# Weight shapes priced in a planner, the first expert's list read before the last block's rows are stored

## The chip, the cores and the metric

The kernel runs on one core of a Trainium2 chip. The metric is the device time of one execution in microseconds; a kernel's time is the median of its runs. The core has five engines that run side by side and meet at semaphores: TensorE (PE; PEld is its weight load), VectorE (DVE), ScalarE (ACT), GpSimd (POOL) and SyncE (SP, which here only issues DMAs).

## What is computed

```python
# q, k, v, f_logit: (4, 8, 768, 48) float32
for t in range(S):                       # gated linear attention
    state = f[:, :, t, :, None] * state + einsum('bhd,bhe->bhde', k[:, :, t], v[:, :, t])
    y[:, :, t] = einsum('bhd,bhde->bhe', q[:, :, t], state)
x = y as 3072 rows of 384                # row = batch * 768 + t
h = x @ w_in                             # dense layer, 384 -> 2048 -> 384
x = (maximum(h, 0) + alpha * minimum(h, 0)) @ w_out
logits = x @ w_gate                      # 8 experts, 384 rows each
for idx in argsort(-logits.flatten()):   # greedy: best pair of row and expert first
    row, e = idx // 8, idx % 8
    if row is free and expert e has fewer than 384 rows: give row to e
out[rows of e] = maximum(x[rows of e] @ w1[e], 0) @ w2[e]   # 384 -> 1024 -> 384
```

## The kernel before

**A planner.** The Python code does not issue instructions directly. A recorder (its one line, L212 before and L215 after, is what the profile shows for nearly all instructions) collects each with what it reads and writes, a modelled cost, and a due time given by `with self.at(...)`. `schedule()` then writes them out engine by engine: at each step the instruction that can start first by the model, ties going to the earlier due time. Where the model sees PE idle, `fill()` puts in products with a matrix `ones` that nobody reads (L1670 before, L1723 after). The order on each engine is therefore fixed when the kernel is built, and a changed constant can move instructions anywhere. `AHEAD` (L47) says how many of the first expert's eight weight tiles are asked for ahead of its gather.

**Attention** runs in 24 chunks. A chunk's products on PE are of three shapes of weights: the k.q products (64 rows by 128 columns of weights, `bank<-early 64*128`), the y products and the state products (128 rows by 64 columns, `128*64`), and transposes by the matrix `ident` and the gate's products, which use the full 128 by 128.

**The dense layer** takes blocks of 384 rows as attention finishes them. Values are split in a high and a low part, so a full-precision product is three PE passes of 384 columns. Eight tiles hold the hidden weights, eight the project weights; each is built early on from the inputs by DVE, ACT and POOL (integer steps on `raw` and `early`, then `weights<-early`, one of whose steps, the split, may go to DVE or POOL as the planner finds). The hidden products are `bank<-rounded,weights`, the project products `bank<-weights,hidden` or, for rows still to be split, `bank<-weights,rounded`. The rows go to a DRAM tensor `x2d` (3072 by 384).

**The experts.** For each expert a chain on DVE and PE finds the threshold of its logits (`seek`, in steps of 12 small PE products `bank<-late 128x16`, one with `pairs`, one with `ok`), takes its rows, and makes a list of their numbers (`lists`: 24 small PE products in three groups of 8, then `idx`). POOL gathers the 384 listed rows from `x2d` with three indirect DMAs, `expert_x` transposes them (three groups of three PE transposes `bank<-ident,common`), and ACT and DVE split them; then come the hidden and the project products. The next expert's chain, list, gather and transposes stand among the products of the expert before it.

**The hand-over** from the dense layer to the first expert: the last block's logits are computed ahead of its rows, so the first expert's list is made while PE still does the last block's 144 project products (`ffn1_rows`). Those rows go to ACT, to `x2d`, and only then may the gather read `x2d`. SP issues, in this order: three weight tiles, the last two stores of rows to `x2d`, a tiny DMA `mark` that waits for the gathered rows, and the other weight tiles.

Of the kernel before, what the change touches and what calls it, by code (L numbers as in the profile page):

```python
# [32 lines left out]
BT = 3  # L33
BK = BT * C
NB = NT // BT
SEG = C + 1
# [13 lines left out]
AHEAD = 3  # L50
# [29 lines left out]
URGENT = 80.0  # L80
WINDOW, BUSY = 10240 / 3, 3060.0
# [53 lines left out]
class Op:  # L135
    def __init__(self, idx, engines, calls, prio):
# [3 lines left out]
        self.extra = 0.0  # L140
# [5 lines left out]
class Plan:  # L146
# [59 lines left out]
    def record(self, engines, method, a, k, slack=0.0):  # L206
# [121 lines left out]
    def schedule(self):  # L328
# [12 lines left out]
        mm, hw, dma = [0.0, 0.0], 600.0, [0.0, 0.0]  # L341

# [23 lines left out]
        for _ in ops:  # L366
# [267 lines left out]
class Kernel:  # L634
# [28 lines left out]
    def constants(self, cp):  # L663
# [19 lines left out]
        with self.at(PAIRS):  # L683
# [31 lines left out]
        nc.gpsimd.iota(self.jpv[:, :, 1], pattern=[[0, NT]], base=0, channel_multiplier=1,  # L715
                       allow_small_or_imprecise_dtypes=True)
# [183 lines left out]
    def s2(self, i):  # L900
        nc, a = self.nc, self.A[i]
        n = HP * SEG
        for name, dec in (("k", a["qr"][:, 1:n + 1].rearrange("p (g t) -> p g t", g=HP)[:, :, 1:]),
# [3 lines left out]
            nc.vector.tensor_tensor(t, a[name], dec, OP.mult)  # L907

# [15 lines left out]
    def s3k(self, i):  # L924
# [6 lines left out]
        for g in range(HP):  # L931
            nc.tensor.transpose(p[:, g * 128:(g + 1) * 128], a["kT"][:, g, :], self.ident)
# [33 lines left out]
    def s4s(self, i):  # L966
# [5 lines left out]
        for g in range(HP):  # L972
            for s in range(2):
                r = slice(s * 64, s * 64 + 64)
# [123 lines left out]
    def ffn1_rows(self, G, store):  # L1098

        for t in range(BT):  # L1100
# [5 lines left out]
            store(t, r, None)  # L1106

# [261 lines left out]
    def lists(self, idx, pos, acc):  # L1369

        nc, wp = self.nc, self.rp
        g = wp.tile([128, NT, 3], F32, name="pg", bufs=1)
# [24 lines left out]
        nc.vector.tensor_scalar(idx, pp, float(N - 1), None, op0=OP.min)  # L1397
# [46 lines left out]
    def gather(self, idx):  # L1444
        xg = [self.gw.tile([128, DM], F32, name="g", bufs=3) for a in range(3)]
        for a in range(3):
            self.nc.gpsimd.indirect_dma_start(out=xg[a], out_offset=None, in_=self.x2d,
# [62 lines left out]
    def flag(self):  # L1510
# [3 lines left out]
        ok = self.rp.tile([128, HP + E], BF, name="okp", bufs=1)  # L1514
        nc.vector.tensor_scalar(ok[:, :HP], self.pmin, PMIN, None, op0=OP.is_ge)
        nc.vector.tensor_scalar(ok[:, HP:], self.inc[:, :, NT - 1], float(CAP), None, op0=OP.is_equal)
        p = self.bank()
        nc.tensor.matmul(p[:, :HP + E], self.ones, ok, start=True, stop=True)
        s = self.rp.tile([128, 1], F32, name="oks", bufs=1)
        nc.vector.tensor_reduce(s, p[:, :HP + E], axis=AX.X, op=OP.add)  # L1520
        self.bad = self.cp.tile([128, 1], I32, name="bad")
        nc.vector.tensor_scalar(self.bad, s, 128.0 * (HP + E) - 0.5, None, op0=OP.is_lt)
# [329 lines left out]
```

## Time and profile before

| | |
|---|---|
| median of 3 runs | 847.98 us (847.36 to 849.97) |
| profiled execution, its own time | 851.19 us |
| its span in the trace | 849.30 us |
| granted PE clock, mean | 0.989 of full speed |
| PE busy | 820.0 us, 97% |
| DVE busy | 564.8 us, 66% |
| ACT, POOL busy | 349.6, 113.9 us |

The profiled execution is 3.21 us above the median, and its time holds 1.89 us outside the span. [...]

### The profile page before, as it was taken

Reading aid. Unit: us, or ns where it says so; the run is one execution under the profiler, and the core shown is the slowest. Engines: PE = TensorE matmul, PEld = TensorE weight load, DVE = VectorE, ACT = ScalarE, POOL = GpSimd, SP = SyncE. Lnnn points to the kernel's source line nnn. Section 1 sums busy time; section 2 is a strip of 40 time slices with the busy share of each in tenths; the row PEclk is TensorE's granted clock in tenths of the full one; section 3 lists DMA queues with packets and bytes.
Section 4 is the critical chain, followed back from the end, with each engine's and each line's share of the span. In section 5 each row is a group of like instructions: output and inputs, shape, how many; then the busy total and the mean of one; then the engine's idle time right before and its main releaser. Section 6 shows DMA issues by size and latency. Waiting matters only on the chain. (4 is left out here: it accounts for less than half of the span.)

```text
span 849.3 us, 16038 instructions
## 1 busy us (share of the span) xinstructions
PE 820.0 (97%) x6122; PEld 756.5 (89%) x6122; DVE 564.8 (66%) x1308; ACT 349.6 (41%) x742; POOL 113.9 (13%) x105
## 2 busy tenths in 40 slices
PE   6999989999999999999999999999999999999995
PEld 3687889999999999999999999888788999899995
DVE  6899976977866966966975754655767658452220
ACT  3577665355555355555455443420122212222220
POOL 3111011210200200300300000000202302311211
PEclk7999999999999999999999999999999999999998
DMA  8895202599889688988878770003878775687400
GB/s 177 221 315 135 48 20 75 136 289 281 231 274 292 136 291 256 236 278 279 248 237 290 251 240 29 1 10 134 312 277 329 316 288 183 246 314 230 164 28 33
DMA packets 92792, 172.60 MB, mean 203 GB/s; under 512 B 31674, under 2 KB 61378, under 8 KB 92706
## 3 DMA queue, kind: packets, MB, share of 16 engines
q1 hardware_dynamic: 89490, 162.04, 60.0%
q0 software_dynamic: 3072, 9.44, 3.2%
q8 instruction: 50, 0.82, 0.4%
q14 instruction: 36, 0.29, 0.1%
q10 hardware_dynamic: 144, 0.01, 0.0%
HBM read 111.69 MB, written 59.77 MB: 202 GB/s over the span
## 5 line engine op out<-in xcount | busy, mean ns | idle before, releaser
L212 PE MATMUL bank<-rounded,weights 128*128 128x384 f32 (+1 forms) x1740 | 354.4, 344 | 1.2 <-POOL weights L212 0.5
L212 PE MATMUL bank<-weights,rounded 128*128 128x392 f32 (+1 forms) x1620 | 325.1, 344 | 3.0 <-ACT weights L212 2.3
L212 PEld LDWEIGHTS bank<-rounded,weights 128*128 128x128 f32 (+1 forms) x1740 | 302.4, 187 | 7.7 <-issue 2.3
L212 PEld LDWEIGHTS bank<-weights,rounded 128*128 128x128 f32 x1620 | 287.5, 189 | 5.6 <-issue 3.2
L212 ACT ACTIVATE rounded<-bank 128x384 fp32r<-128x384 f32 x110 | 54.1, 492 | 201.1 <-PE bank L212 188.4
L212 DVE TENSOR_TENSOR early<-early 128x384 fp32r<-128x384 f32 (+2 forms) x196 | 120.0, 629 | 16.1 <-ACT early L212 15.1
L212 PEld LDWEIGHTS bank<-early 128*64 128x64 f32 (+2 forms) x1696 | 98.3, 153 | 20.9 <-issue 10.4
L212 PE MATMUL bank<-early 128*64 128x128 f32 (+3 forms) x1696 | 110.2, 269 | 2.7 <-DVE early L212 1.5
L212 DVE SCALAR_TENSOR_TENSOR common<-common,rest,bank 128x384 f32<-128x384 f32 x128 | 77.9, 608 | 47.1 <-ACT common L232 46.1
L212 ACT ACTIVATE early<-early 128x384 fp32r<-128x384 f32 (+2 forms) x177 | 95.4, 548 | 31.9 <-DMA wd<-early 20.4
L212 POOL TENSOR_TENSOR rounded<-common,rounded 128x384 fp32r<-128x384 f32 x36 | 49.4, 1373 | 435.0 <-ACT rounded L212 398.0
L232 ACT ACTIVATE common<-bank 128x384 f32<-128x384 f32 x128 | 62.6, 489 | 71.4 <-PE bank L212 70.9
L212 ACT ACTIVATE rounded<-common 128x384 fp32r<-128x384 f32 x118 | 62.0, 525 | 65.9 <-DVE common L212 62.8
L212 DVE SCALAR_TENSOR_TENSOR rounded<-bank,rounded 128x384 fp32r<-128x384 f32 x62 | 34.5, 556 | 50.2 <-ACT rounded L212 48.3
L212 DVE TENSOR_TENSOR rounded<-common,rounded 128x384 fp32r<-128x384 f32 x82 | 46.5, 566 | 28.7 <-ACT rounded L212 20.3
L212 DVE TENSOR_TENSOR_SCAN early<-early 128x516 f32<-128x516 f32 x48 | 61.9, 1289 | 1.9 <-ACT early L212 1.6
L212 ACT ACTIVATE common<-bank 128x384 f32<-128x384 f32 x48 | 23.3, 492 | 71.4 <-PE bank L212 69.7
L212 POOL DMA_INDIRECT out_dram<-common,late x24 | 25.5, 1061 | 167.8 <-ACT common L212 115.7
L212 DVE TENSOR_TENSOR late<-late,cols 128x1536 bf16<-128x1536 bf16 (+3 forms) x53 | 42.7, 817 | 0.2
L212 POOL DMA_INDIRECT common<-x2d,late x24 | 25.9, 1077 | 90.2 <-DVE late L212 58.6
L212 DVE TENSOR_TENSOR rounded<-bank,rounded 128x384 fp32r<-128x384 f32 x48 | 26.3, 555 | 10.8 <-ACT rounded L212 10.3
L212 DVE TENSOR_TENSOR early<-bank,mask 128x512 f32<-128x512 f32 x48 | 31.0, 684 | 3.2 <-PE bank L212 2.9
(110 smaller groups left out, 488.7 us busy)
## 6 DMA issues: line engine op xcount, KB each, us to landing
wd<-early SPq DMA_DIRECT2D x128, 384.0 KB
weights<-wd SPq DMA_DIRECT2D x64, 768.0 KB
early<-in_w_dram SPq DMA_DIRECT2D x64, 384.0 KB
early<-in_fkq_dram SPq DMA_DIRECT2D x46, 288.0 KB
raw<-in_w_in_dram SPq DMA_DIRECT2D x16, 384.0 KB
raw<-in_w_out_dram SPq DMA_DIRECT2D x16, 384.0 KB
early<-in_v_dram SPq DMA_DIRECT2D x24, 192.0 KB
x2d<-common SPq DMA_DIRECT2D x24, 192.0 KB
```

Source lines behind the costliest of these rows:

```text
L212: op = self.add(engines, lambda e, b: getattr(e, method)(*[b(x) for x in a], **{n: b(x) for n, x in k.items()}), outs, ins)
L232: return e.activation(b(out), b(x), AF.Relu, scale=-1.0)
```

## The change

Two things are changed. First, the planner learns what a change of the weights' shape costs on PE: an instruction's `form` is the number of rows of its weights and whether they have 64 columns, and a PE instruction whose form differs from the one before it is priced at `TURN` more, with `LONGER` and `AGAIN` for a neighbour. The state products now also wait, in the planner, until the chunk's y products are issued (`a["done"]`), and the transposes of `kT` until the chunk's scaled rows are made (`a["rows"]`). Second, the first expert's gather no longer waits for the last block's rows. `x2d` gets one more row, of zeros, at 2688 (`NE`), and the last block's 384 rows are stored one row further on. The list for the first expert points every row of the last block at the zero row, reads only rows 0 to 2688, and the last block's rows are added by PE: `picks` are three 128 by 128 matrices of zeros and ones, and `first_x` sums, for the third 128 columns, the gathered rows times `ident` and each of the three blocks of fresh rows times its `picks`. That is right as long as the first expert takes at least 256 of its rows from earlier blocks, which one more term of the kernel's flag looks at. Every expert's list now makes two vectors, `idx` and `tok`, the second with the shift by one row taken back out for the scatter. `AHEAD` becomes 2.

```diff
+NE = N - BK
-AHEAD = 3
+AHEAD = 2
+TURN, LONGER, AGAIN = 92.0, 72.0, 80.0
...
+            op.form = ins[0].ap[0][1], free_size(ins[0]) == 64
...
+                t, again = t + again, 0.0
+                turn = TURN if op.form != form else LONGER if short and price > 130.0 else 0.0
+                if turn:
+                    t, again = t + turn, AGAIN
+                form, short = op.form, price <= 130.0
...
+        a["rows"] = self.last(2)
...
-        for g in range(HP):
-            nc.tensor.transpose(p[:, g * 128:(g + 1) * 128], a["kT"][:, g, :], self.ident)
+        with self.behind(a["rows"]):
+            for g in range(HP):
+                nc.tensor.transpose(p[:, g * 128:(g + 1) * 128], a["kT"][:, g, :], self.ident)
...
+            with self.behind(a["done"]):
                 nc.tensor.matmul(p[r, g * D:(g + 1) * D], a["kt"][:, g, r], a["v"][:, 2 * g + s, :D], start=True, stop=True)
...
+            rows.append(r)
+        return rows
...
-        nc.vector.tensor_scalar(idx, pp, float(N - 1), None, op0=OP.min)
+        nc.vector.tensor_scalar(idx, pp, float(NE if first else N), None, op0=OP.min)
+        if first:
+            r3 = wp.tile([128, BT], F32, name="r3", bufs=1)
+            nc.vector.scalar_tensor_tensor(r3, g[:, NT - BT:, 2], -128.0, r[:, NT - BT:], op0=OP.mult, op1=OP.add)
+            self.picks = wp.tile([128, BT, 128], F32, name="picks", bufs=1)
+            for t in range(BT):
+                nc.vector.tensor_scalar(self.picks[:, t], self.cols[:, :, 0], r3[:, t:t + 1], None, op0=OP.is_equal)
+        t = wp.tile([128, 3], F32, name="pt")
+        nc.vector.tensor_scalar(t, pp, NE + 0.5, -1.0, op0=OP.is_ge, op1=OP.mult)
+        nc.vector.scalar_tensor_tensor(tok, pp, float(N), t, op0=OP.min, op1=OP.add)
+        return idx, tok
...
+    def first_x(self, xg, rows):
+        x = [self.xp.tile([128, KD, CAP], F32R, name="x" + s, bufs=2) for s in "HL"]
+        for a in range(2):
+            self.split_x(x, a, xg[a], self.bank())
+        p = self.bank()
+        parts = [(rows[t], self.picks[:, t]) for t in range(BT)]
+        parts.insert(BT - 1, (xg[2], self.ident))
+        for n, (w, m) in enumerate(parts):
+            for kd in range(KD):
+                cols = slice(kd * 128, (kd + 1) * 128)
+                self.nc.tensor.matmul(p[:, cols], w[:, cols], m, start=(n == 0 and kd == 0), stop=True, skip_group_check=True)
+        self.halve_x(x, 2, p)
+        return x
...
-            self.x2d = dp.tile([N, DM], F32, name="x2d")
+            self.x2d = dp.tile([N + 1, DM], F32, name="x2d")
...
-                nc.sync.dma_start(self.x2d[j * 128:(j + 1) * 128], r)
+                at = j * 128 if j < NT - BT else j * 128 + 1
+                nc.sync.dma_start(self.x2d[at:at + 128], r)
...
         with self.at(ROWS):
-            self.ffn1_rows(G, store(NB - 1))
+            rows = self.ffn1_rows(G, store(NB - 1))
         with self.at(GATHER0):
-            xg = self.gather(idx)
+            xg = self.gather(idx, NE + 1)
             nc.sync.dma_start(self.mark, xg[2][:1, :16])
             here = self.last(1)
-            ready = idx, self.expert_x(xg)
+            ready = tok, self.first_x(xg, rows)
```

What this does to the order of instructions is shown at three places.

**PE, end of the last block.** Before, behind the last project products of the block and two steps of the chain, fillers and the first expert's transposes (`ident,common`) stand in turn; these rows come after the second step's 12 products, and the tile `weights_419` that follows a third step holds the first expert's first weights:

```order
L1670 LDWEIGHTS ones
L1670 MATMUL bank_73<-ones 128x512
L212 MATMUL bank_66<-ident,common 128x128 x3
L212 MATMUL bank_67<-late,pairs 128x8
L212 MATMUL bank_68<-ident,common 128x128 x3
L212 LDWEIGHTS ones
L212 MATMUL bank_67<-ok_83,ones 128x1
```

Now two groups of transposes and the product of the gathered third by `ident` stand inside the last block's project products (`weights_1054` to `weights_1291` are the last three project tiles):

```order
L215 MATMUL bank_69<-weights_1054,hidden 128x384 x4
L215 MATMUL bank_67<-ident,common 128x128 x3
L215 MATMUL bank_69<-weights_1054,hidden 128x384 x2
L215 MATMUL bank_69<-weights_1175,hidden 128x384 x2
L215 MATMUL bank_68<-ident,common 128x128 x3
L215 MATMUL bank_69<-weights_1175,hidden 128x384 x3
L215 MATMUL bank_66<-ident,common 128x128 x3
L215 MATMUL bank_69<-weights_1175,hidden 128x384
L215 MATMUL bank_69<-weights_1291,hidden 128x384 x6
```

Behind the last project product and the 12 products of the chain's first step, only this stands ahead of the first expert's hidden products (`weights_435` is its first weight tile now):

```order
L1723 LDWEIGHTS ones
L1723 MATMUL bank_73<-ones 128x512
L215 MATMUL bank_66<-late,common 128x128 x3
L215 MATMUL bank_68<-late,pairs 128x8
L1723 LDWEIGHTS ones
L1723 MATMUL bank_73<-ones 128x512
L1723 LDWEIGHTS ones
L1723 MATMUL bank_73<-ones 128x512
L215 LDWEIGHTS ones
L215 MATMUL bank_67<-ok_83,ones 128x1
L215 MATMUL bank_72<-rounded,weights_435 128x384 x9
```

The first gather's transposes moved from behind the last block into it, the last block's own rows enter by three products (`late,common`) behind it, and the chain's second and later steps moved from ahead of the first expert's products to among them.

**PE, the last of the eight hidden weight tiles, first use.** It is `weights_1277` before and `weights_1235` after. Before:

```order
L212 MATMUL bank_69<-weights_1150,rounded 128x392 x3
L212 MATMUL bank_70<-weights_1150,rounded 128x392 x3
L212 MATMUL bank_71<-weights_1150,rounded 128x392 x3
L212 MATMUL bank_72<-rounded,weights_1277 128x384 x9
L212 MATMUL bank_73<-rounded,weights_1277 128x384 x9
```

After:

```order
L215 MATMUL bank_68<-early 64x128 x20
L215 MATMUL bank_67<-early 128x8 x2
L215 MATMUL bank_72<-rounded,weights_1235 128x384 x9
L215 MATMUL bank_67<-early 128x8
L215 MATMUL bank_66<-ident,early 128x128 x3
L215 MATMUL bank_68<-ident,early 128x128 x3
L215 MATMUL bank_69<-weights_962,rounded 128x392
```

Ahead of that first use PE has 234 products of the dense layer before and 207 after, and 7 gate products and 6 transposes fewer.

**DVE, the second expert's list.** From the list's first copy out of PSUM, before (the first `late<-late 128x3` is `idx`, which releases the gather):

```order
L212 COPY late<-bank_68 128x3
L212 TENSOR_SCALAR late<-late,mid,fine 128x24
L212 SCALAR_TENSOR_TENSOR late<-bank_68,late 128x3
L212 TENSOR_REDUCE late<-late 128x24
L212 TENSOR_SCALAR late<-late 128x3
```

After (the last row is `tok`, which releases the gather):

```order
L215 COPY late<-bank_66 128x3
L215 TENSOR_SCALAR late<-late 128x24
L215 SCALAR_TENSOR_TENSOR late<-bank_66,late 128x3
L215 TENSOR_TENSOR late<-late,cols 128x1536
L215 TENSOR_SCALAR late<-late 128x3 x2
L215 SCALAR_TENSOR_TENSOR rounded<-bank_73,rounded 128x384
L215 SCALAR_TENSOR_TENSOR late<-late 128x3
```

A comparison over 1536 columns and a split of a hidden tile moved in front of the vector that the gather waits for.

## Rows read from the trace of the kernel before

**Rows 1.** Page, part 1: busy time of each engine, share, instructions.

```profile
PE 820.0 (97%) x6122; PEld 756.5 (89%) x6122; DVE 564.8 (66%) x1308; ACT 349.6 (41%) x742; POOL 113.9 (13%) x105
```

**Rows 2.** Windows: length; busy us (instructions) of PE, PEld, DVE, ACT, POOL; clock; DMA share; GB/s.

```profile
100.00:120.00 20.00, 17.56 (x108) 16.70 (x107) 18.68 (x39) 16.21 (x41) 3.05 (x3) 1.00 0.03 7
120.00:140.00 20.00, 20.00 (x127) 19.25 (x125) 9.41 (x23) 10.31 (x26) 0.73 (x1) 1.00 0.21 70
```

**Rows 3.** Waits of PE: what it waited for, us in total, times, longest us.

```profile
PE bank L212 <- DVE early L212: 7.6, 5, 5.6
PE bank L212 <- DMA common<-x2d,late: 2.9, 3, 1.9
```

**Rows 4.** Timeline of PE at 209 to 217 us: start, us, line, output<-inputs, count.

```profile
209.48 2.40 PE L212 MATMUL bank<-early 128*64 128x128 f32 x40
211.81 0.45 PE L212 MATMUL bank<-rounded,weights 128*128 128x384 f32 x1
212.19 1.16 PE L212 MATMUL bank<-early 64*128 64x128 f32 x16
213.28 1.32 PE L212 MATMUL bank<-rounded,weights 128*128 128x384 f32 x6
214.53 2.40 PE L212 MATMUL bank<-early 128*64 128x128 f32 x40
```

**Rows 5.** Timeline, end of the weight preparation, several engines.

```profile
106.20 1.01 POOL L212 TENSOR_TENSOR rounded<-common,rounded 128x384 fp32r<-128x384 f32 x1 [6.46 <-ACT weights L212]
...
106.30 1.32 DVE L212 SCALAR_TENSOR_TENSOR early<-raw,early 128x384 int32<-128x384 int32 x1
...
107.55 0.55 DVE L212 SCALAR_TENSOR_TENSOR early<-early,raw 128x384 int32<-128x384 int32 x1
...
116.26 0.95 PE L212 MATMUL bank<-early 128*128 128x8 f32 x8
...
119.07 0.54 DVE L212 TENSOR_TENSOR weights<-early,weights 128x384 fp32r<-128x384 f32 x1
...
121.00 3.34 PE L212 MATMUL bank<-rounded,weights 128*128 128x384 f32 x18
```

**Rows 6.** Timeline from the first expert's list to its first hidden products.

```profile
583.19 0.17 DVE L212 TENSOR_SCALAR late<-late 128x3 int32<-128x3 f32 x1
...
583.58 5.37 PE L212 MATMUL bank<-weights,hidden 128*128 128x384 f32 x30
...
588.79 0.46 PE L212 MATMUL bank<-late 128*128 128x16 bf16 x12
...
592.43 1.12 POOL L212 DMA_INDIRECT common<-x2d,late  x1 [58.56 <-DVE late L212]
...
595.84 0.49 PE L212 MATMUL bank<-ident,common 128*128 128x128 f32 x3
...
599.00 0.49 ACT L212 ACTIVATE rounded<-bank 128x384 fp32r<-128x384 f32 x1 [0.55 <-PE bank L212]
...
599.75 1.41 PE L212 MATMUL bank<-rounded,weights 128*128 128x384 f32 x6
```

**Rows 7.** Timeline, second expert's gather and first transposes.

```profile
610.55 0.95 DVE L212 TENSOR_TENSOR late<-late,cols 128x1536 bf16<-128x1536 bf16 x1
...
610.79 1.53 POOL L212 DMA_INDIRECT common<-x2d,late  x1 [14.72 <-DVE rounded L212]
...
619.52 0.87 PE L212 MATMUL bank<-ident,common 128*128 128x128 f32 x3 [1.88 <-DMA common<-x2d,late]
```

**Rows 8.** Windows around that gather (columns as in rows 2).

```profile
615.00:620.00 5.00, 3.12 (x29) 2.54 (x28) 1.66 (x7) 0.49 (x1) 0.00 (x0) 0.96 1.02 400
620.00:625.00 5.00, 5.00 (x35) 4.65 (x34) 2.98 (x7) 1.48 (x3) 0.00 (x0) 0.70 1.03 420
```

**Rows 9.** Timeline, third expert's first transposes.

```profile
646.20 0.49 PE L212 MATMUL bank<-ident,common 128*128 128x128 f32 x3
```

**Rows 10.** Timeline of PE, seventh expert's second transposes.

```profile
770.21 0.55 PE L212 MATMUL bank<-ident,common 128*128 128x128 f32 x3 [0.68 <-DMA common<-x2d,late]
```

More of the change, by code (lines that the diff above doesn't have):

```diff
@@ L714, in constants @@
                        allow_small_or_imprecise_dtypes=True)
-        nc.gpsimd.iota(self.jpv[:, :, 1], pattern=[[0, NT]], base=0, channel_multiplier=1,
-                       allow_small_or_imprecise_dtypes=True)
+        zero = cp.tile([128, DM // 128], F32, name="zero")
+        nc.gpsimd.memset(zero, 0.0)
+        with self.at(PAIRS):
+            nc.sync.dma_start(self.x2d[NE:NE + 1].rearrange("o (p c) -> p (o c)", c=DM // 128), zero)
+        for j, n in ((0, NT - BT), (NT - BT, NT)):
+            nc.gpsimd.iota(self.jpv[:, j:n, 1], pattern=[[0, n - j]], base=int(j > 0), channel_multiplier=1,
+                           allow_small_or_imprecise_dtypes=True)
         self.lg = cp.tile([128, NT, E], F32, name="lg")
@@ L971, in s4s @@
         p = self.bank()
-        for g in range(HP):
-            for s in range(2):
-                r = slice(s * 64, s * 64 + 64)
+        for g, s in [(g, s) for g in range(HP) for s in range(2)]:
+            r = slice(s * 64, s * 64 + 64)
+            with self.behind(a["done"]):
                 nc.tensor.matmul(p[r, g * D:(g + 1) * D], a["kt"][:, g, r], a["v"][:, 2 * g + s, :D], start=True, stop=True)
@@ L1098, in ffn1_rows @@
     def ffn1_rows(self, G, store):
+        rows = []
         for t in range(BT):
@@ L1367, in take, with lists @@
         self.pos, self.acc, self.ei = pos, W, ei
-    def lists(self, idx, pos, acc):
+    def lists(self, pos, acc, first=False):
         nc, wp = self.nc, self.rp
+        idx, tok = wp.tile([128, 3], I32, name="idx", bufs=E), wp.tile([128, 3], I32, name="tok", bufs=E)
         g = wp.tile([128, NT, 3], F32, name="pg", bufs=1)
@@ L1442, in expert_weights, with gather @@
             self.plan.add(("sync",), lambda e, b, i=i, t=t: e.dma_start(b(t.bitcast(F32)), source(i, reg[0])), [t], [self.wd], 60.0, 128 * 1536 * 4, [get])
-    def gather(self, idx):
+    def gather(self, idx, rows=None):
         xg = [self.gw.tile([128, DM], F32, name="g", bufs=3) for a in range(3)]
         for a in range(3):
-            self.nc.gpsimd.indirect_dma_start(out=xg[a], out_offset=None, in_=self.x2d,
+            self.nc.gpsimd.indirect_dma_start(out=xg[a], out_offset=None, in_=self.x2d if rows is None else self.x2d[:rows],
                                               in_offset=bass.IndirectOffsetOnAxis(ap=idx[:, a:a + 1], axis=0))
@@ L1513, in flag @@
         nc = self.nc
-        ok = self.rp.tile([128, HP + E], BF, name="okp", bufs=1)
+        ok = self.rp.tile([128, HP + E + 1], BF, name="okp", bufs=1)
         nc.vector.tensor_scalar(ok[:, :HP], self.pmin, PMIN, None, op0=OP.is_ge)
-        nc.vector.tensor_scalar(ok[:, HP:], self.inc[:, :, NT - 1], float(CAP), None, op0=OP.is_equal)
+        nc.vector.tensor_scalar(ok[:, HP:HP + E], self.inc[:, :, NT - 1], float(CAP), None, op0=OP.is_equal)
+        nc.vector.tensor_scalar(ok[:, HP + E:], self.inc[:, 0, NT - BT - 1:NT - BT], CAP - 128.0, None, op0=OP.is_ge)
         p = self.bank()
-        nc.tensor.matmul(p[:, :HP + E], self.ones, ok, start=True, stop=True)
+        n = HP + E + 1
+        nc.tensor.matmul(p[:, :n], self.ones, ok, start=True, stop=True)
         s = self.rp.tile([128, 1], F32, name="oks", bufs=1)
-        nc.vector.tensor_reduce(s, p[:, :HP + E], axis=AX.X, op=OP.add)
+        nc.vector.tensor_reduce(s, p[:, :n], axis=AX.X, op=OP.add)
         self.bad = self.cp.tile([128, 1], I32, name="bad")
-        nc.vector.tensor_scalar(self.bad, s, 128.0 * (HP + E) - 0.5, None, op0=OP.is_lt)
+        nc.vector.tensor_scalar(self.bad, s, 128.0 * n - 0.5, None, op0=OP.is_lt)
     def scan_pair(self, ap, b, g, xd):
@@ L1632, in general @@
                     self.expert_weights(1, self.ei)
-                    idx = self.rp.tile([128, 3], I32, name="idx")
-                    self.lists(idx, self.pos, self.acc)
-                    self.expert(1, idx, self.expert_x(self.gather(idx)))
+                    _, tok = self.lists(self.pos, self.acc)
+                    self.expert(1, tok, self.expert_x(self.gather(tok)))
     def main(self, ctx):
@@ L1793, in record @@
                 with self.at(base + LISTS):
-                    idx = self.rp.tile([128, 3], I32, name="idx", bufs=E)
-                    self.lists(idx, *was[:2])
-                    ready = idx, self.expert_x(self.gather(idx))
+                    idx, tok = self.lists(*was[:2])
+                    ready = tok, self.expert_x(self.gather(idx))
             self.wide = p == E - 1
```

8 lines of the change are left out of this document (4 added, 4 removed).

## Prediction

> **What bounds the kernel now.** I read the page first: PE is busy 820.0 us of 849.3, DVE 564.8 [rows 1]. An average over stages hides which of them waits, so next come windows of 20 us. Up to about 122 us DVE is the full one, 18.68 of 20 with PE at 17.56; then PE is at 20.00 and DVE falls to 9.41 [rows 2]. So two regimes: while weights are prepared the end is set by DVE, and from there on by PE. The list of PE's waits confirms it: the largest, 7.6 us, is on DVE's `early` tiles, the next, 2.9 us, on gathered rows [rows 3]. Then the timeline of two places: the attention chunks in the PE-bound part, for what a change of shape costs, and the hand-over, for what stands between the last block and the first expert.
>
> **Turns.** In program order PE's changes of weights' shape fall from 124 to 112. From the place on where PE is the bound they fall from 86 to 80; the other six lie in the DVE-bound stretch and I give them nothing there. A plain pass of 384 columns takes 5.21/30 = 0.174 us (30 of them from 583.58 to 588.79) [rows 6]. The single one at 211.81 takes 0.38 until the next starts, the six at 213.28 take 1.25 where 1.04 would do [rows 4]: coming back to the full shape costs 0.2. What going into a small shape costs can't be told from these rows; the 40 products at 209.48 start the next 2.33 later, 0.058 each, which leaves room for nothing up to about another 0.2. I take 0.1, so 0.3 for a pair of changes, and three pairs give **-0.9**, bounds -0.5 and -1.5.
>
> **Early stretch.** PE first uses the last hidden tile after 207 products of the dense layer, where it was 234: 27 x 0.174 = 4.7 us less. With 7 gate products (8 records in 0.95, 0.12 each, two to a product: 1.7) and 6 transposes (0.12 each, 0.7) that is 7.1 us less PE work in front of it [rows 5]. DVE's work in front of that tile shrinks less. By the order of instructions it loses two integer steps (0.55 each), one eviction (0.55), three tiny steps (0.17 each, as the list's last row [rows 6]) and three splits of weights (0.54 each, moved to POOL) [rows 5]: 3.8 us. The tile was ready at 119.61 and used at 121.00, a slack of 1.4 [rows 5]. So PE comes 7.1 - 3.8 - 1.4 = 1.9 us too soon. A wait there can also stand in for one of PE's other waits on DVE, of which 7.6 us exist. [...]
>
> **Hand-over.** The list of the first expert is there at 583.19, but the gather goes out at 592.43, behind the stores of the last block's rows; the transposes start at 595.84, ACT's last split at 599.00, and the first hidden product at 599.75, 10.96 us after 588.79, when the last project product is through [rows 6]. After the change the gather can go at about 584. The transposes that it feeds start 3.4 us behind its issue (592.43 to 595.84 before), so now its rows are there near 588, covered by the project products that last to 588.79. Into that stretch go 6 transposes (0.12 each, as above: 0.7) and 9 full-precision products (two records each, 0.24 at most; I take 0.22: 2.0). I add 1.2 for waits: the picks are made by three new DVE steps between the list's PE groups, and six of the nine products and the list's third group stand behind them. The project products then end at 588.8 + 2.7 + 1.2 = 592.7. Behind them come ACT's eviction (0.49, and twice 0.25 to be told and to tell, as between 599.49 and 599.75), the last three products (0.65), and ACT's split (0.49): first hidden product at 594.85 [rows 6]. That is **-4.9**; bounds -6.5 (no waits, nothing but the products) and -3.
>
> **Chain.** Before, the second, third and fourth steps of the next expert's chain ran while PE had fillers. Now three groups of 12 products stand among the first expert's products, 0.46 us each [rows 6]: **+1.4**. The SP queue behind it: the first weight tiles are asked for sooner, because `mark` waits for rows that land some 10 us sooner; two tiles ahead instead of three costs nothing while six more have those 7 us to come, and without that cover a tile is 768 KB, 2.0 us at the 400 GB/s of [rows 8]. The last store of rows now stands behind these tiles on SP, ahead of the second expert's tiles, whose number is known later still.
>
> **Later gathers.** The gather of each next expert now waits for `tok`. For the second expert the order on DVE puts a 1536-column comparison (0.95 [rows 7]) and one split (0.55) in front of it: 1.5 us later. PE has one product fewer between list and transposes, 0.2. [...] For the others the steps on DVE in front of `tok` are counted in the same way. The third's is 0.85 later; its transposes had no wait at 646.20 [rows 9], so the slack is unknown, and I take +0.8. The fourth to sixth are 0.45 later and have one to three products (about 0.25 us) fewer, and no wait: nothing. The seventh is 0.6 later and waits already [rows 10]: +0.6. Sum **+2.6**, bounds 0 and 5.4.
>
> Other edits: one DMA of a row of zeros, one more column in the flag, eight times two tiny DVE steps. Among the experts DVE is busy for 1.66 and 2.98 of 5 us [rows 8], so they hide under PE's products; uncovered, they would be 16 x 0.17 = 2.7 us [rows 6].
>
> **Sum.** -0.9 + 1.0 - 4.9 + 1.4 + 2.6 = **-0.8** on the profiled execution, whose own time is 851.19. That run lies 3.2 above the median of 847.98; the difference is put on the median: **847.2**. What can be told from no change is 0.3%, 2.5 us: 845.4 to 850.5.
>
> **Rivals.** (a) The later gathers don't come later in effect: the first expert's tiles are through sooner and leave the queues free when the second expert's gather is issued, so `tok`'s lateness is hidden. For it: the gather at 610.79 took 8.7 us against 3.4 for the first one, and the difference is the weights beside it. Against it: the second expert's tiles come in the same stretch. Without that term the sum is -3.4: **844.6**. (b) All gathers come late: 1.7 for the second, 1.05 for the third, 0.7 for each of the next three, 0.6 for the seventh, 5.4 in all, and one more stretch at half clock, as the clock's 0.96 and 0.70 over five us each [rows 8] cost before: 5 x 0.04 + 5 x 0.30 = 1.7. That is 7.1, 4.5 above the term: **851.7**, slower. It decides where these stops together pass 5.9 us, for then the sum is +2.5. (c) The early stretch is the full 1.9, and POOL's splits hurt DVE: beside a POOL step that reads two tiles at 106.20 a DVE step took 1.32 where it takes 0.55 at 107.55 [rows 5], so two splits that meet such steps add 1.6. Then the stretch costs 3.5 instead of 1.0: **849.7**. (d) The change doesn't do what it says: the picks are late, PE stops inside the last block for what it stopped for behind it, and only 2 of the 4.9 come: **850.1**.
>
> [...]
>
> **Chances.** The forecast has 0.33, of which 0.07 lie below 845.4, where turns and early stretch are at their lower bounds. (c) alone has 0.09 and (d) 0.06, and both end within 0.3%: 0.26 + 0.09 + 0.06 = 0.41 for no change that can be told. (a) has 0.30, so faster is 0.37. (b) has 0.15 and (c) together with late gathers 0.07: slower 0.22. The likeliest's own range is 845.4 to 850.5. The range reaches to (a) with the turns at their end and a better early stretch, 843.0, and to (b), 851.7.
>
> **What the profile after would show.** The first expert's hidden products start 2 to 3 us behind the last project product, where it was 10.96, and that product ends some 4 us later than the list of before would have it; no row of fillers stands between chain steps. Transposes of the second expert behind a stop of 2 to 4 us on the gathered rows: right; a stop under 1 us: (a). PE's wait for the weight tiles of the eighth pair: none or up to 2 us, over 3 is (c). Passes behind 122 us at 0.174 with fewer returns. [...]

## The result, and the profile after

The changed kernel, called after below, takes 853.55 us (median of 6 runs, 852.70 to 856.97) against 848.25 (6 runs, 847.36 to 849.97): a ratio of 1.0061, 95% interval 1.0043 to 1.0080. It is slower, where no change that can be told was forecast, 847.2, and the time lies outside the range that was given. Ratios below are against runs of the kernel before on the same chip, where its median was 845.59 to 849.30 us; so kernels of different runs are compared by ratio. The profiled execution took 852.90, with a span of 851.1.

The page, part 1, after (compare [rows 1]):

```profile
PE 816.8 (96%) x6103; PEld 754.1 (89%) x6103; DVE 567.5 (67%) x1333; ACT 352.1 (41%) x742; POOL 103.3 (12%) x103
```

PE has 3.2 us less to do and the span is 1.8 longer: time went into PE's standing still. The list of its waits says on what (compare [rows 3]):

```profile
PE bank L215 <- DVE early L215: 10.1, 8, 4.5
PE bank L215 <- DMA common<-x2d,late: 4.5, 11, 0.9
PE bank L215 <- DVE weights L215: 2.3, 3, 1.4
PE bank L215 <- DVE late L215: 2.2, 6, 0.6
```

Waits on `early` rose from 7.6 to 10.1, waits on gathered rows from 3 of 2.9 us together to 11 of 4.5. The windows around the end of the preparation (compare [rows 2]):

```profile
100.00:120.00 20.00, 18.88 (x150) 17.50 (x150) 16.52 (x33) 13.46 (x34) 2.52 (x2) 1.00 0.06 11
120.00:140.00 20.00, 20.00 (x126) 18.87 (x125) 8.18 (x21) 10.35 (x26) 0.00 (x0) 1.00 0.21 70
```

DVE is through sooner, 16.52 instead of 18.68, but that helps only if PE is as far on then. The timeline of the hand-over (compare [rows 6]):

```profile
586.02 1.12 POOL L215 DMA_INDIRECT common<-x2d,late  x1 [50.92 <-DVE late L215]
...
589.22 0.55 PE L215 MATMUL bank<-ident,common 128*128 128x128 f32 x3 [0.28 <-DMA common<-x2d,late]
...
591.11 0.52 PE L215 MATMUL bank<-ident,common 128*128 128x128 f32 x3 [0.65 <-DMA common<-x2d,late]
...
592.47 0.94 PE L215 MATMUL bank<-ident,common 128*128 128x128 f32 x6 [0.32 <-DMA common<-x2d,late]
...
594.47 0.46 PE L215 MATMUL bank<-late 128*128 128x16 bf16 x12
...
595.21 0.94 PE L215 MATMUL bank<-late,common 128*128 128x128 f32 x6
...
596.72 1.92 PE L215 MATMUL bank<-rounded,weights 128*128 128x384 f32 x9
```

The hand-over is nearly as forecast: the project products end at 594.47, the first expert's hidden products start 2.25 us behind them, where it was 10.96, and 3.0 us sooner in all. The second expert's gather (compare [rows 7]) is issued at 616.85, and PE stands for each of its thirds:

```profile
624.24 0.55 PE L215 MATMUL bank<-ident,common 128*128 128x128 f32 x3 [0.32 <-DMA common<-x2d,late]
...
625.72 0.55 PE L215 MATMUL bank<-ident,common 128*128 128x128 f32 x3 [0.37 <-DMA common<-x2d,late]
...
626.93 0.55 PE L215 MATMUL bank<-ident,common 128*128 128x128 f32 x3 [0.20 <-DMA common<-x2d,late]
```

**A second execution of the kernel before.** The prediction was summed on an execution of 851.19. A second one took 846.71. Windows of 5 us (busy us, then clock, DMA share, GB/s) show where they part, first the first execution, then the second:

```profile
10.00:15.00 5.00, 2.00 (x7) 1.16 (x7) 2.96 (x8) 0.85 (x2) 0.00 (x0) 0.70 1.19 266
15.00:20.00 5.00, 5.00 (x39) 3.54 (x39) 3.21 (x8) 3.12 (x7) 0.00 (x0) 0.50 0.85 204
20.00:25.00 5.00, 5.00 (x36) 2.80 (x35) 3.38 (x8) 0.61 (x2) 0.00 (x0) 0.77 0.02 3
```

```profile
10.00:15.00 5.00, 1.92 (x7) 1.06 (x7) 2.88 (x8) 0.85 (x2) 0.00 (x0) 0.82 1.16 259
15.00:20.00 5.00, 5.00 (x46) 3.17 (x45) 3.55 (x9) 3.12 (x7) 0.00 (x0) 0.84 0.91 214
20.00:25.00 5.00, 5.00 (x66) 3.73 (x65) 4.84 (x11) 3.17 (x7) 0.00 (x0) 1.00 0.40 88
```

From 5 to 15 us PE was busy for 4.4 us in the first and 4.9 in the second. Behind that the first ran longer at a granted clock of 0.50, by the windows above 10.3 us against 3.4 (the traces of before and after hold clocks of 1.00 and 0.50 alone, so a mean between them is time spent at each); the first product of the dense layer starts at 41.76 in the one and 39.17 in the other. The same order of instructions thus gives times 2.7 us apart at product 600 by its start alone (the first one's other 1.9 us come among the experts), and one profile is a poor base for a few us.

For all runs I took from their traces three stretches: up to product 600 of the dense layer (all preparation lies in it), products 600 to 2220 (PE-bound, attention between products), and the rest (hand-over and experts). The first line is the second execution of before in us, the others are the differences from it; `115` is the time of products 1565 to 1680, a stretch with nothing between them.

```
run                         to 600   600-2220   rest    115    profiled
before, second execution     215.7      350.7   278.4   20.43   846.71
before, first                 +2.7       -0.1    +1.9   20.43   851.19
after                         +2.5       +0.7    +3.0   20.31   852.90
planner alone                 +5.0       +1.9    +5.5   20.43   859.18
list alone                    +1.6       -1.8    +1.9   20.31   848.33
AHEAD 3                       +2.4       +0.7    +0.9   20.31   850.64
prices alone                  +7.9       +4.0    +8.7   20.43   867.34
waits alone                   +6.1       -0.9    +0.4   20.43   852.52
shifted                       +3.6       -1.5    +0.8   20.31   849.55
list and waits                +6.1       -2.1    +0.7   20.31   851.72
late waits, shifted           -0.4       -2.6    -1.0   20.31   842.63
late prices                   -0.2       +4.1    +7.4   20.43   857.95
shifted twice                 +6.3       -0.4    +0.7   20.39   853.25
list, not shifted             -1.2       -0.7    +5.2   20.40   849.96
list, late waits, gathers 1st -1.6       -2.6    -1.0   20.31   841.40
list, late waits              -1.7       -2.7    +1.8   20.31   844.16
late waits, shifted, again    +1.4       -2.5    +0.7   20.31   846.20
```

The middle column repeats within 0.2 us for one order and one placement. The first ranges from -1.7 to +6.3 for kernels that have before's order up to the end of the preparation, and it goes with the time that PE spent at a granted clock of 0.50 before product 600: 3 us in the runs from -1.7 to 0, 7 at -0.4, 10 from +1.4 to +2.7, 17 at +3.6, 24 at +6.3. Differences there are read from the order and from the medians.

### The profile page after: what moved, and what is told of

The parts are those of the page before. It is cut to its first block, busy times and chain, and to the rows that moved or that the text cites. A ratio compares the mean times of both kernels' runs of the same rounds, so it can differ in the third digit from the quotient of the medians.

```text
span 851.1 us, 16003 instructions
## 1 busy us (share of the span) xinstructions
PE 816.8 (96%) x6103; PEld 754.1 (89%) x6103; DVE 567.5 (67%) x1333; ACT 352.1 (41%) x742; POOL 103.3 (12%) x103
## 5 line engine op out<-in xcount | busy, mean ns | idle before, releaser
L215 PE MATMUL bank<-rounded,weights 128*128 128x384 f32 x1740 | 355.1, 344 | 0.8 <-POOL weights L215 0.6
L215 PEld LDWEIGHTS bank<-rounded,weights 128*128 128x128 f32 x1740 | 302.1, 188 | 7.9 <-issue 1.3
L215 PEld LDWEIGHTS bank<-early 128*64 128x64 f32 (+2 forms) x1696 | 100.6, 153 | 24.3 <-DVE early L215 12.9
L215 POOL TENSOR_TENSOR rounded<-common,rounded 128x384 fp32r<-128x384 f32 x29 | 36.4, 1257 | 439.9 <-ACT rounded L215 410.3
L215 DVE TENSOR_TENSOR rounded<-common,rounded 128x384 fp32r<-128x384 f32 x89 | 50.7, 570 | 34.8 <-ACT rounded L215 29.2
```

The source lines that it names most:

```text
L215: op = self.add(engines, lambda e, b: getattr(e, method)(*[b(x) for x in a], **{n: b(x) for n, x in k.items()}), outs, ins)
```

## The experiments

Theory A: the loss comes from the planner's part, that is from its order in attention. Theory B: it comes from the early list, at the hand-over and among the experts.

**The kernel before once more** (no edit). 

> The kernel before, profiled a second time. Its first profiled execution took 851.19 us against a median of 848.25, and held a stop of 1.88 us on the second expert's gathered rows followed by a stretch at a granted clock of 0.70. If that episode is what lifts an execution above the median, a profile with a time near 848 has no such stop, and its first hidden product of the second expert comes 3 us sooner after the first expert's. If an execution near 848 holds the episode too, the surplus lies elsewhere.

846.71 us. It also has a stop on the second expert's rows, of 1.54 us. So the surplus of the first was not that stop alone: 2.6 us had come at the start.

**The planner's part alone**, before with (the lines that apply the prices are those of the change)

```diff
+TURN, LONGER, AGAIN = 92.0, 72.0, 80.0
...
+        a["rows"] = self.last(2)
...
+        with self.behind(a["rows"]):     # transposes of kT
...
+            with self.behind(a["done"]): # state products
```

> The kernel before with the prices of turns and the two waits in the planner, and nothing else (AHEAD 3, the list and gather as before). Theory A (the loss is in the attention part, where the new order makes PE and DVE wait): 852 to 854 us, ratio 1.004 to 1.007. Theory B (the loss is in the hand-over and the experts, where the chain's steps and gathers now stand among the products): 847 to 849 us, ratio 0.998 to 1.001.

860.10 us, ratio 1.0167 (1.0134 to 1.0200): more than twice the loss of the whole change. **The list alone**, after with

```diff
-TURN, LONGER, AGAIN = 92.0, 72.0, 80.0
+TURN, LONGER, AGAIN = 0.0, 0.0, 0.0
...
-        with self.behind(a["rows"]):
+        with self.behind(()):
...
-            with self.behind(a["done"]):
+            with self.behind(()):
```

> The changed kernel with all prices of turns at 0 and without the two waits in the planner: only the early list, the picks, the zero row and AHEAD 2 are left. Theory A: 846 to 848 us (the hand-over's gain of about 3 us less what the gathers give back). Theory B: 851 to 854 us.

848.16 us, ratio 1.0021 (0.9994 to 1.0047). So the loss comes with the planner's part, as theory A has it, and not with the list. But attention, A's place for it, has only half of it: of the planner's +12.5 us in the profile 5.5 lie behind product 2220, where attention is done; and 860.10 is well above the 852 to 854 that A allowed. Besides, the two are not a sum: 1.67% and 0.21% apart make 0.61% together, since every edit has the planner write a new order. **After with AHEAD 3**:

```diff
-AHEAD = 2
+AHEAD = 3
```

> The changed kernel with AHEAD 3: three instead of two of the first expert's weight tiles are asked for ahead of its gather. If the gather's rows were late because of weights, this makes it later (up to 2 us, one tile of 768 KB); if the weights of the first expert are what is late, it makes the kernel up to 2 us faster. Theories A and B both have the stop elsewhere: 853 to 854.5 us, ratio to the kernel before 1.005 to 1.008.

852.40 us, ratio 1.0075 (1.0045 to 1.0106), not told apart from after. No cost of that edit can be told, as priced; the intervals leave room for 2 us less to 4 us more.

**The planner's two halves.** Prices alone (the first line of the planner's part with the lines that apply it, on before), and the waits alone (its other three). 

> The kernel before with the prices of turns alone (no waits in the planner, list as before). In its order PE's changes of weights' shape are 129, where before has 124, and fillers fall from 97 to 79. Theory P (the prices misplace instructions in the first 140 us, where PE then stands and its clock falls): 854 to 860 us, most of the loss of the planner's whole part (+14). Theory W (the two waits hold back state products that the recurrence needs): 845 to 848 us.

> The kernel before with the two waits in the planner alone (prices 0, list as before): 108 changes of shape instead of 124, 95 fillers. Theory P: 843 to 846 us, since eight pairs of changes at 0.2 to 0.3 us lie in PE's path, -1.6 to -2.4 against the kernel before. Theory W: 854 to 860 us.

The prices alone: 865.81 us, 1.0169 (1.0136 to 1.0202), slow in all three stretches. The waits alone: 852.02, 1.0037 (1.0014 to 1.0060). Theory P holds in that the prices are the larger part, more than the 854 to 860 that it allowed; but the waits aren't the gain that it wanted: 0.9 us less in the PE-bound stretch, and more up to product 600. The traces show why. In before's order PE has 96.0 us of work left up to product 600 when the last weight is prepared; with the waits it has 100.0, with the prices 98.7, after 99.8 (prepared at 118.5, product 600 at 218.3). The weights come no more than 1.2 us sooner, the work behind them is some 4 us more.

**After without the prices** (the first pair of lines of the list alone's diff). 

> The changed kernel with the prices of turns at 0: list, picks and the two waits are left, 108 changes of shape. Theory P: the time of the list alone (1.002 of before) less 1.6 to 2.4 us: 844 to 846.5 us, ratio 0.998 to 1.001. Theory W: slower than the list alone by 6 or more: over 853 us.

851.87 us, 1.0027 (1.0008 to 1.0045): slower than the 846.5 that P allowed, though 2.1 us less in the PE-bound stretch. As with the waits alone more is left when the last weight is prepared, 101.0 us.

**A constant that nobody reads**, before with

```diff
+        zero = cp.tile([128, DM // 128], F32, name="zero")
+        nc.gpsimd.memset(zero, 0.0)
```

> The kernel before with one unused constant of 128 by 3 numbers put among the constants, so that whatever is placed after it in SBUF lies one step further; the order on every engine stays. In the dense layer's plain stretches 115 products took 20.43 us in the kernel before and in the run with the planner's part alone, 20.31 in all runs with the list. If the place in SBUF does that, this run shows 20.31 and 3 to 4 us less in all (842 to 843); if not, 20.43 and the time of the kernel before within 0.3%.

846.46 us, 0.9959 (0.9937 to 0.9982), and 115 products in 20.31: with one order of instructions, the place in SBUF is worth 0.4%, 3.5 us. An estimate from the plain stretch fits: 3468 products at 0.12/115 us each make 3.6. **Two of them** (the same two lines again, as `more`): 

> The kernel before with two unused constants of 128 by 3 numbers, so that what is placed after them lies two steps of 32 bytes further; the order stays. If what matters is which half of 64 bytes a tile begins in, the plain stretch of 115 products takes 20.43 us again and the time is that of the kernel before (ratio 0.999 to 1.001). If any shift helps: 20.31 and ratio 0.996.

847.98 us, 0.9987 (0.9968 to 1.0007), 20.39. Most of the gain is gone, though 20.39 isn't 20.43; which places do it stays open.

**The list alone with `more` added**, so that it isn't shifted by one step. 

> The run with the list alone and one more unused constant, so that SBUF places are again a whole 64 bytes off those of before. The order of the list alone is that of before up to the hand-over. If the list's whole gain in the plain stretches was the shift, 115 products take 20.43 us here and the ratio is 1.0021 + 0.004 = 1.006 (1.004 to 1.009): then the list itself, the hand-over's 4 us included, costs about 5 us among the experts. If the list is neutral: 1.000 to 1.003.

849.64 us, 1.0011 (0.9991 to 1.0031), 20.40: inside the band for a neutral list, and against the kernel shifted twice 0.24% slower, which the two intervals leave open. The rest is +5.2 in its profile although the hand-over is shorter than in after.

**Where the waits and the prices cost.** Before with the unused constant and the waits only behind the preparation, whose chunks are the first six:

```diff
+        with self.behind(a["rows"] if i >= 2 * BT else self.plan.waits if self.plan else ()):
+            with self.behind(a["done"] if i >= 2 * BT else self.plan.waits if self.plan else ()):
```

> The kernel before with the unused constant of the shifted run and with the two waits in the planner for the chunks from the seventh on alone; the order on PE and DVE is that of before up to the end of the weight preparation, behind it there are 8 changes of shape fewer. If the waits cost only in the preparation (there: about 4 us more PE work left when it ends), this is the shifted run less 8 changes at 0.09 to 0.14 us: ratio 0.994 to 0.996, 842 to 845 us against a kernel before of 848. If they also cost later: ratio above 0.998.

845.62 us, 0.9954 (0.9933 to 0.9975); once more on another chip 846.13, 0.9958 (0.9935 to 0.9981). 

> The fast run once more, on the same chip as the two with the list: 0.9954 again, between 0.993 and 0.998.

The waits cost only in the preparation. Behind it they save 1.0 us beyond the shift's part in the PE-bound stretch (-2.6 against -1.5). Prices only behind the preparation, on before:

```diff
-                turn = TURN if op.form != form else LONGER if short and price > 130.0 else 0.0
+                turn = 0.0 if t < 130000.0 else TURN if op.form != form else LONGER if short and price > 130.0 else 0.0
```

> The kernel before with the prices of turns applied only where the planner's clock is past 130 us; the order up to the end of the weight preparation is that of before. In the run with the prices everywhere the products 600 to 2220 of the dense layer took 354.7 us where before took 350.7, with attention products at 74.0 instead of 68.3 us. If the prices cost by what they do in the PE-bound part, ratio 1.004 to 1.008 with that 4 us; if only by the first 140 us, ratio 0.999 to 1.001.

858.91 us, 1.0134 (1.0104 to 1.0165), above what was expected: +4.1 in the PE-bound stretch and +7.4 behind it. The prices cost behind the preparation too, so the first 140 us, theory P's place, hold the smaller part. Of the 7.4 behind product 2220 a part are stops on gathered rows (3.6 to 6.1 us among the experts in the three kernels with prices and the old list, 1.4 to 2.9 in the seven executions with that list and no prices); the rest was not traced. One place in the PE-bound stretch, from the timeline:

```profile
274.65 0.44 PE L214 MATMUL bank<-rounded,weights 128*128 128x384 f32 x1
...
276.00 1.26 DVE L214 TENSOR_TENSOR early<-bank,mask 128x512 f32<-128x512 f32 x2
...
276.20 0.67 PE L214 MATMUL bank<-early 128*64 128x48 f32 x16 [1.11 <-DVE early L214]
```

One product of the dense layer stands between two visits (runs of attention's products), and then PE waits 1.11 us for DVE; in before's order more products stand there. Over products 600 to 2220 the spacings that have to do with attention sum to 68.3 us in before, 74.0 with the late prices and 71.7 after. In the same stretch the changes of shape are 54 in before, 58 with the prices and 56 after: they rise.

After has no stop on `early` there. Its 3.4 us more stand, for 2.9 of them, between a product of the dense layer and the product of another kind behind it (13.3 us in before, 16.2 after). Ahead of attention such a spacing is mostly 0.27 us, but 0.35 to 0.47 where one product of the dense layer stands alone between two visits; after, for instance:

```profile
266.54 0.42 PE L215 MATMUL bank<-rounded,weights 128*128 128x384 f32 x1
266.98 0.43 PE L215 MATMUL bank<-early 128*64 128x128 f32 x2
267.34 0.44 PE L215 MATMUL bank<-rounded,weights 128*128 128x384 f32 x1
267.71 1.98 PE L215 MATMUL bank<-early 128*64 128x128 f32 x38
```

Over products 600 to 2220 there are 5 such single products in before, none with the late waits, 10 after and 19 with the late prices.

**The hand-over's gain.** The kernel with late waits, with list, picks and AHEAD 2 added; and the same with one more wait in the planner (`puts` is filled where the scatters are issued, not shown):

```diff
+        got = set(self.last(3))        # the three gathers
+        for o in self.puts:            # second and third scatter of the expert before
+            o.soft.update(got)
```

> The same without the wait for the scatters: the fast run plus the list, picks and AHEAD 2. POOL has a scatter between the gathers for the third and the fourth expert. If the list costs what the two pairs of runs showed (0.24% and 0.62%, about 3.5 us): ratio 0.998 to 1.001 where the fast run has 0.9954.

> The fast run (unused constant, waits from the seventh chunk on, prices 0) with the list, picks and AHEAD 2 of the changed kernel, and with one more wait in the planner: an expert's second and third scatter stand behind the next gather on POOL, so no scatter stands between the three gathers. If the scatters between the gathers are what ate the hand-over's 4 us, PE's waits on gathered rows among the experts fall from 6.5 to 2 or 3 us and the time is 3 us or more below the same without the wait, ratio 0.990 to 0.994. If it is the chain, which now stands among the products: no difference between the two, both 0.998 to 1.001.

846.15 us, 0.9969 (0.9944 to 0.9993) without that wait, 841.29 us, 0.9901 (0.9880 to 0.9921) with it. POOL's timeline at the fourth expert's gather, without:

```profile
659.55 1.47 POOL L215 DMA_INDIRECT common<-x2d,late  x1 [3.53 <-PE bank L215]
661.33 0.95 POOL L215 DMA_INDIRECT common<-x2d,late  x1 [0.30 <-PE bank L215]
664.35 0.99 POOL L215 DMA_INDIRECT out_dram<-common,late  x1 [2.08 <-DMA out_dram<-common,late]
665.64 0.97 POOL L215 DMA_INDIRECT common<-x2d,late  x1 [0.30 <-issue]
```

And PE, which comes for that third part:

```profile
672.71 0.52 PE L215 MATMUL bank<-ident,common 128*128 128x128 f32 x3 [2.15 <-DMA common<-x2d,late]
```

With it:

```profile
660.19 0.99 POOL L215 DMA_INDIRECT common<-x2d,late  x1 [3.90 <-PE bank L215]
661.49 0.98 POOL L215 DMA_INDIRECT common<-x2d,late  x1 [0.30 <-PE bank L215]
662.77 0.95 POOL L215 DMA_INDIRECT common<-x2d,late  x1 [0.30 <-issue]
664.93 1.00 POOL L215 DMA_INDIRECT out_dram<-common,late  x1 [1.22 <-issue]
```

A scatter (`out_dram`) that stands between the gathers waits 2.08 us for the scatter before it, and the third gather behind it is issued 3 us later and PE stops 2.15 us for its rows. PE's waits on gathered rows behind 565 us, without the wait and with it:

```profile
PE bank L215 <- DMA common<-x2d,late: 4.9, 6, 2.1
```

```profile
PE bank L215 <- DMA common<-x2d,late: 2.4, 3, 1.5
```

That is 2.5 us, and the two rests differ by 2.8 (1.8 and -1.0). Behind the stop of 2.15 us the granted clock falls as well, to 0.76 where it is 1.00 with the wait (windows of 5 us, columns as in [rows 2]), first without the wait, then with it:

```profile
675.00:680.00 5.00, 5.00 (x35) 4.59 (x34) 2.09 (x7) 0.49 (x1) 0.00 (x0) 0.76 0.01 4
```

```profile
675.00:680.00 5.00, 5.00 (x30) 5.00 (x29) 4.97 (x20) 0.98 (x2) 0.00 (x0) 1.00 0.78 289
```

The medians differ by 4.9, more than the profiles (2.8): all six runs with the wait had a mean granted clock of 0.992 or more, only six of the twelve without it, and the median of those six is 843.67, 2.4 above. So the wait is worth 2 to 3 us, and the rest of the 4.9 may be the clock of the start. This is the fastest version tried, 0.99% below the kernel before; some of that may be the clock, too.

## Why the prediction was wrong

By stretch, in us, the forecast and what the profile of after shows against the two executions of before:

| stretch | forecast | against the second | against the first |
|---|---|---|---|
| to product 600 (early stretch) | +1.0 | +2.5 | -0.1 |
| 600 to 2220 (turns) | -0.9 | +0.7 | +0.8 |
| 2220 to the first expert's first hidden product (hand-over) | -4.9 | -3.5 | -3.8 |
| from there to the end (chain, later gathers) | +4.0 | +6.5 | +4.8 |
| sum | -0.8 | +6.3 | +1.8 |

**Turns: the step that failed.** I counted the changes of shape that vanish, priced them, and took the count for the whole effect of the planner's prices. The price was a little high: in the traces a dense product ahead of attention takes 0.27 us instead of 0.18, and the first one behind it starts 0.15 to 0.20 after the last attention product, where those start 0.05 apart; so a pair costs 0.19 to 0.24, and I had 0.3. But the count doesn't carry the effect. The late waits save 1.1 us over products 300 to 2220 with 8 changes fewer, 0.14 each on average, yet seven of the eight lie in products 300 to 600, where they brought less than 0.1. And the changes didn't vanish where I had put them: from 86 to 80 holds, but as 32 to 24 in products 300 to 600 and 54 to 56 in 600 to 2220. What failed is that prices are also the planner's clock. With them it cuts the dense layer's products into other pieces, twice as many single ones between two visits of attention; and the stretch takes 0.7 us more in spite of a shift worth 1.5, so +2.2 where I had -0.9. Prices alone make 1.69%, and taking them out of the changed kernel takes 1.0061 to 1.0027 (that the waits then still cost is the early stretch below). Why PE takes longer behind a single product the rows don't tell. A planner's cost is no property of one term; what an added cost moves elsewhere has to be priced as well.

**Early stretch: right in mechanism, low in size.** PE does less in front of the last hidden tile, so more is left behind: 99.8 us instead of 96.0. Of the 7.1 us less work 3.8 remain as a loss less 1.2 that the weights came sooner, 2.5 in the profile, where I had 1.0 and (c) 3.5. The 1.0 was my estimate, half of the 1.9 by which PE was to come too soon; no run shows it, and the profile has the 2.5 in its place. PE's waits on DVE's `weights` rose from 0.4 to 2.3 us. That the waits belong to it wasn't in my count; limiting them to later chunks took the list from 1.0027 to 0.9969.

**Hand-over: right in mechanism.** -4.9 forecast; the first hidden product is 3.0 sooner and the project products started 0.7 later, so -3.7, inside the bounds. I had allowed 1.2 for waits on the picks; PE waited for none. It stopped instead for the first gather's rows (0.28, 0.65, 0.32), which I had as covered: the list took until 584.91 and the gather went at 586.02, not 584. The missing 1.2 comes with the prices, too: from product 2220 to the first expert's first hidden product it takes 27.0 and 27.2 us in the two kernels with list and prices, 25.6 to 25.8 in the five with the list and without prices, where PE stops once, for 0.6 or 0.7, and 30.5 and 30.8 in before. Without the prices the 4.9 are there.

**Chain and later gathers: the sum near, its parts wrong.** From the first expert's first product to its last, after takes 4.3 us more than the first execution of before (245.0 against 240.7), where chain and gathers were priced at 1.4 + 2.6 = 4.0. That this fits is luck. The six other executions with the old list and no prices take 237.6 to 238.9, so against them 6.1 to 7.4 are lost. And the loss doesn't lie at the gathers: the spacings in front of their transposes, stops included, sum to 12.3 us in the first execution, 12.9 in the second and 12.7 after. Those in front of the chain's and the lists' small products sum to 28.4, 25.1 and 33.3. So the term of the chain, +1.4, was too small by 3 to 7 us, and of that of the gathers, +2.6, nothing is seen (-0.2 to +0.4). Its largest part, 1.2 for the second expert, was my estimate from the stop of 1.88 in [rows 7] and 1.7 of lateness; no run shows it, and PE stopped there for 0.32, 0.37 and 0.20. PE, held up by the chain, may also come later for the rows. The chain's spacings differ by 3 us between two executions of one order, so one profile doesn't give its size better. Which of PE's order, DVE and the queues makes them wait in after was not tried apart.

I also had the gathers of the second to the eighth expert wait for `tok`, and so says the last of the lists of instructions ahead of the prediction. They read `idx`, one step earlier; only the scatter uses `tok`. The third expert's gather is issued before `tok` is made:

```profile
639.92 0.99 POOL L215 DMA_INDIRECT common<-x2d,late  x1 [1.95 <-PE bank L215]
...
640.43 0.15 DVE L215 SCALAR_TENSOR_TENSOR late<-late 128x3 int32<-128x3 f32 x1
```

What remains of that term is the 0.95 us comparison in front of the second expert's `idx`. In the four kernels with the list, without prices and without the wait for the scatters, a scatter stands between two gathers of the third and of the fourth expert, and PE stops for rows among the experts for 4.0 to 6.1 us, where both executions of before have 2.9. After has no such scatter, and 3.3.

**The base.** I moved the median by a sum made on one execution 3.2 us above it. Between the profiles the change costs 1.7, between the medians 5.3: the first execution hides 3.6 of the 6 us by which I missed. Against the second execution of before, 2.7 of the first one's surplus lie at its start and 1.9 among the experts; no term of mine could show that. So the column against the second execution is the one to go by.

**The rivals.** (a) By the sign that I named for it, a stop under 1 us at the second expert, it came: 0.32, 0.37 and 0.20 where 1.88 had been, and the clock stays at 1.00 in every window of 5 us from 600 to 675. Its time, 844.6, didn't come, because the loss lay elsewhere. (b) had the right sign and time, 851.7, but neither its late gathers nor its half clock came. (c), 849.7, had the early stretch; whether a POOL step lengthens a DVE step beside it, as the 1.32 us against 0.55 in [rows 5] let me think, was not tried apart. Three more splits of weights are on POOL, 7 where 4 had been, as counted, and POOL's busy time over the whole fell from 113.9 to 103.3. (d) didn't come: 3.7 of the 4.9 are there. Both (b) and (c) together, to which I gave 0.07, were nearest in time, not in cause.

## What to carry to other kernels

Where a planner sets the order, an edit is worth what the new order is worth: run its price, its wait and the data path apart before believing a sum of terms, and look for the stretch in which each acts. A sum made on one execution should be set against a second one of the same kernel first. A change that makes one engine's stream better can leave more of it behind the moment that bounds it: here 99.8 us instead of 96.0 when the last weight is prepared. Let nothing that waits stand between transfers that an engine is about to need: on POOL one scatter between the gathers waited 2.08 us, the gather behind it was issued 2.87 later, and PE stopped 2.15 for its rows.

## What was not expected of the hardware

A constant of 128 by 3 numbers that nobody reads, placed ahead of the working tiles, makes the same products start closer together: hidden products 175.6 instead of 176.6 ns apart, project products 177.7 instead of 179.6. 115 of them take 20.43 us without it, 20.31 with one, 20.39 with two, and with one the kernel is 0.41% faster. The changed kernel had that gain by accident (its row of zeros), so the rest of the change cost more than 1.0061 says. Why the spacing goes with the place in SBUF no run shows. And one order of instructions reached product 600 within a range of 8 us, with 3 to 24 us at a granted clock of 0.50 in its first 125 us from one execution to another.
